# Delta-rule attention with routed experts: first scores from plain keys, small PSUM results in spare columns, routing in two stages

## The chip, the cores and the metric

The kernel runs on one core of a Trainium2 chip, in float32 throughout. The metric is device time in microseconds (us), less is better. Names of engines: PE is the tensor engine's matmul side and PEld its weight loads, DVE the vector engine, ACT the scalar engine, POOL the general engine, SP the engine whose queue issues most transfers. PSUM, where matmuls write, has eight banks of 512 float32 columns on 128 partitions.

## The reference

Two parts follow each other. The first is a delta-rule attention over 4 batches, 8 heads, 768 tokens, width 48; the second sends each of the 3072 tokens (8 heads side by side, 384 columns) to the one expert of eight with the highest logit.

```python
k_n = k / (norm(k) + 1e-6)
for t in range(S):
    y[:, :, t] = q[t] @ state
    v_old = state @ k_n[t]
    state = state + beta[t] * outer(k_n[t], v[t] - v_old)
x = y as (3072, 384)
logits = x @ w_gate
e = argmax(logits); gate = softmax(logits)[e]
out = gate * (relu(x @ w1[e]) @ w2[e])
```

## The kernel before

**The attention in chunks.** Tokens are handled in 24 chunks (steps) of 32 tokens, all four batches and eight heads of a chunk together: batch b lies on partitions 32b to 32b+31. For each chunk `scores` (L207) multiplies the keys with keys and queries into a PSUM tile `pa`, and `keep_scores` (L223) has DVE mask it into `gt` (keys) and `qk` (queries), two instructions on L235. Two heads share a partition range of 64 each, and to keep them apart the right-hand operand is a "wide" copy `wkq` with zeros in the other head's place, loaded by `load_wide` (L190) on top of the plain tile `kq`. There are three wide buffers, so a load of chunk c+3 waits for the matmuls of chunk c.

**The inversion.** Four chunks make a group. `invert` (L241) works on DVE alone: it normalises the keys, then inverts a triangular 32 by 32 matrix for each head, token and batch by about 30 pairs of a product (L324) and a sum (L329), and writes `ub` with four transposes (L336). It is a generator that yields after each instruction or two. For the first group only two 16-wide diagonal blocks are inverted, and the block across is made by PE: `across` (L350) multiplies (L358), ACT copies the result to `m` (L363), `second` multiplies again (L372) and DVE adds (L377). These are queued as chores.

**A step.** `begin(c)` (L407) takes the PSUM pair of banks `pc` and lets PE write the scaled values into its first bank (L411). `step(c)` (L417) then issues, in this order on PE: keys by state onto the same bank (L425), which ACT copies to R (L436); three transposes of the previous chunk's output (`turn`, L505); ub by R into the second bank of pc (L442), copied by ACT to Z (L447); queries by state into `pq` (L425); logits of the previous chunk (L521); sometimes one more score; qk by Z onto pq (L462), copied by ACT to `xg` (L472) and stored to the tensor xs; keys by Z onto the four banks `acc` (L478), from which ACT writes the states for the next step (L486). Between these ACT scales the next chunk's values (`scale_v`, L391). L425 of the next step needs the states.

**Who comes when.** The order on each engine is the order in which the Python code issues the instructions (the schedule is manual). `fill(us)` (L167) issues DVE instructions from the generators `soon` (routing) or `behind` (inversions) until an estimated number of microseconds is used up; two inversions at hand are issued in turn. The loop (L655 to L673) does a step, up to two chores, a score (`more`), `begin` of the next step, `fill(2.0)`, `fill(4.6)`, and only then the masks of that score. At each fourth step it first issues what is left of the inversion that the step needs (L656 to L658).

**PSUM.** acc takes four banks, pc two, pq one, and psA has one bank for everything else (L143): scores `pa`, the tile `po` of `across`, and the tile `pt` of `turn`, which holds the transposes, the logits (columns 384 to 391) and the ranks (from column 448). A new tile in psA waits until the one before has been read.

**Routing.** Once four chunks have logits (three and one at the end), `route` (L531) finds the best expert on DVE, has ACT take the exponential (L559) and makes the gate (L563 to L567, stored by SP on L568); `ranks` (L574) counts by two matmuls (L578), `listed` (L584) works out each token's place and POOL scatters the token numbers into lists (L605).

**The front.** Eight chunks (FRONT) are scored ahead of step 0, with a few matmuls without use (`heat`, L399) between. SP issues each key tile with its wide loads; values and keys by token of chunks 0 and 1 (`load_vt`, `load_kt`) are issued after the eight scores' loads (L646 to L648).

**The experts.** After the last step and its routing come 24 more heats, then for each expert a gather of its token rows on POOL (L722), transposes (L741), first product (L750), second product (L766) and a scatter of the output (L730).

Of the kernel before, what the change touches and what calls it, by code (L numbers as in the profile page):

```python
# [22 lines left out]
C = 32  # L23
# [17 lines left out]
FRONT = 8  # L41
RK = DM + 64
# [5 lines left out]
def _f32_consts():  # L48

    p = np.arange(128)[:, None]
    j = np.arange(128)[None, :]
    rev = np.broadcast_to(E - np.arange(E), (128, E))
    base = np.broadcast_to(np.arange(E) * LIST, (128, E))
    more = np.arange(E)[:, None] * LIST + CAP + np.arange(MAXR)[None, :] * 128
    more = np.broadcast_to(more.reshape(1, -1), (128, E * MAXR))
    t, w = p % C, j[:, :C]
    own = t // (C // 2) == w // (C // 2)  # L60
    kk = 1.0 * (t == w) - (t < w)
    k0 = 1.0 * (t == w) - ((t < w) & own) - (t // (C // 2) > w // (C // 2))
    return np.concatenate(
        [rev, base, more, p < j, np.ones((128, 128)), kk, k0, -1.0 * (t < w)], axis=1
    ).astype(np.float32)
# [3 lines left out]
def kernel(  # L69
# [22 lines left out]
    nc.scalar.dma_start(out=cf[:], in_=nc.inline_tensor(fc, name="c_f32").ap())  # L92
    at = [0]

    def part(w):
# [4 lines left out]
    rev, base, further, upper, ones, mask_g, mask_0, mask_q = (  # L100
        part(w) for w in (E, E, E * MAXR, 128, 128, C, C, C)
# [4 lines left out]
    nc.scalar.dma_start(out=wg[:], in_=moe_w_gate.rearrange("(s p) e -> p s e", p=128))  # L106
# [48 lines left out]
    beta = persist.tile([128, NG, C], FP32, name="beta")  # L155
# [3 lines left out]
    turned, counted, ranked = [], [], []  # L159

    behind, soon, chores = deque(), deque(), deque()
# [5 lines left out]
    def fill(us):  # L167


        while us > 0 and (soon or behind):  # L170
            from_ = soon or behind
            n = next(from_[0], None)
            if n is None:
                from_.popleft()
                continue
            us -= (0.09 if from_ is behind and len(behind) > 1 else 0.165) + 0.00104 * n
            if from_ is behind and len(behind) > 1:
                behind[0], behind[1] = behind[1], behind[0]

    def chore(n=1):  # L180
        while n and chores:
            chores.popleft()()
            n -= 1
# [6 lines left out]
    def load_wide(c):  # L190
        if c < NS:
            for e in range(2):

                r = slice(64 * e, 64 * e + (64 if c < 3 else D))
                nc.sync.dma_start(out=wide_kq[c % 3][r, e], in_=kq_t[c, r])
# [11 lines left out]
    def scores(c):  # L207

        if c >= NS:
            return None  # L210
        kq, wide = kqs[c], wide_kq[c % 3]
        pa = psA.tile([128, 512], FP32, name="pa", tag="pa")
        for p in range(NP):
            for b in range(B):
                nc.tensor.matmul(  # L215
                    pa[rows_of(b), 128 * p : 128 * p + 128], lhsT=kq[:, p, 0, rows_of(b)],
                    rhs=wide[:, :, p, :, rows_of(b)], start=True, stop=True, skip_group_check=True,
                )
        load_wide(c + 3)
        load_kq(c + 4) if c < FRONT - 4 else None  # L220
        return pa

    def keep_scores(c, pa):  # L223
# [6 lines left out]
        view = pa[:].rearrange("q (h k w) -> q k h w", h=H, k=2)  # L230
        for out, part, mask in (
            (gts[g][:, H * s : H * s + H, :], view[:, 0], mask_g if g else mask_0),
            (qks[c][:], view[:, 1], mask_q),
        ):
            nc.vector.tensor_tensor(  # L235
                out=out, in0=part, in1=mask.unsqueeze(1).to_broadcast([128, H, C]), op=OP.mult
            )
# [112 lines left out]
    def across(g, s):  # L350
# [3 lines left out]
        po = psA.tile([128, 512], FP32, name="po", tag="pa")  # L354
        for h in range(H):
# [8 lines left out]
            out=m1[:].rearrange("p h w -> p (h w)"), in_=po[:, 0 : H * W], func=AF.Copy  # L364
        )

        def second():
            po = psA.tile([128, 512], FP32, name="po", tag="pa")
            for h in range(H):
                sh = H * s + h  # L370
                for b in range(B):
                    nc.tensor.matmul(  # L372
                        po[rows_of(b), W * h : W * h + W], lhsT=fdt[rows_of(b), sh, :],
                        rhs=m1[rows_of(b), h, :], start=True, stop=True, skip_group_check=True,
                    )
            part = ub[:, H * s : H * s + H, W:C]
            nc.vector.tensor_tensor(  # L377
                out=part, in0=part,
                in1=po[:, 0 : H * W].rearrange("p (h w) -> p h w", h=H), op=OP.add,
# [19 lines left out]
    def heat(n=1):  # L399

        for _ in range(n):
            nc.tensor.matmul(  # L402
                front[0][:, 0, :], lhsT=ident[:],
                rhs=warm[:], start=True, stop=True, skip_group_check=True,
# [12 lines left out]
    def step(c):  # L417
# [15 lines left out]
        else:  # L433
# [5 lines left out]
            turn(c - 1)  # L439
        for h in range(H):  # L440
            for b in range(B):
# [3 lines left out]
                )  # L445
        Z = work.tile([128, H, D], FP32, name="Z")
# [7 lines left out]
        scale_v(c + 1, 0)  # L454
        if turned:
            logits(*turned.pop())
        if scored[0] < min(NS, c + LEAD):
            keep_scores(*score())
        scale_v(c + 1, 1)
        for h in range(H):  # L460
            for b in range(B):
                nc.tensor.matmul(  # L462
                    pq[rows_of(b), D * h : D * h + D], lhsT=qk[rows_of(b), h, :],
                    rhs=Z[rows_of(b), h, :],
                    start=(c == 0 and h == 0), stop=True, skip_group_check=True,
                )
        ss = first[c]
        if c == ss[0]:
            xgs[c] = work.tile([128, GS, ROW], FP32, name="xg")
            lgs[c] = small.tile([128, GS, E], FP32, name="lg")  # L470
        x = xgs[ss[0]][:, c - ss[0], 0:DM]
        nc.scalar.activation(out=x, in_=pq[:, 0:DM], func=AF.Copy, scale=-1.0)  # L472
        nc.sync.dma_start(out=xs[128 * c : 128 * c + 128, 0:DM], in_=x)
        if c < NS - 1:
# [9 lines left out]
            for e in range(2):  # L484
# [4 lines left out]
                )  # L489

# [9 lines left out]
    def turn(c):  # L500

        ss = first[c]
        pt = psA.tile([128, 512], FP32, name="pt", tag="pa")
# [5 lines left out]
        if counted:  # L509
            counted.pop()(pt)  # L510
# [4 lines left out]
        turned.append((c, xT, pt))  # L515

    def logits(c, xT, pt):

        ss = first[c]
        for s in range(NK):  # L520
            nc.tensor.matmul(  # L521
                pt[:, DM : DM + E], lhsT=xT[:, s, :], rhs=wg[:, s, :],
# [3 lines left out]
            out=lgs[ss[0]][:, c - ss[0], :], in_=pt[:, DM : DM + E], func=AF.Copy  # L526
# [4 lines left out]
    def route(ss, xg, lg):  # L531
# [6 lines left out]
        def wide(a):  # L538
# [23 lines left out]
        su = row("su", 1)  # L562
        nc.vector.tensor_reduce(out=su[:], in_=ex[:], axis=AX_X, op=OP.add)  # L563
        yield C
        nc.vector.tensor_scalar(out=su[:], in0=su[:], scalar1=1e-9, scalar2=None, op0=OP.add)
        yield C
        nc.vector.reciprocal(out=xg[:, 0:n, DM], in_=su[:])  # L567
        nc.sync.dma_start(  # L568
            out=xs.rearrange("(c p) r -> p c r", p=128)[:, ss[0] : ss[0] + n, DM],
            in_=xg[:, 0:n, DM],  # L570
        )
        yield C

        def ranks(pt):  # L574
# [7 lines left out]
            ranked.append(listed(pt))  # L582

        def listed(pt):  # L584
            pr = small.tile([128, 2 * GS * E], FP32, name="pr")
            nc.vector.tensor_copy(out=pr[:, 0 : 2 * n * E], in_=pt[:, RK : RK + 2 * n * E])
            yield C
# [26 lines left out]
    for c in range(GS):  # L614
        load_kq(c)
        if c < 3:
            load_wide(c)
    nc.scalar.dma_start(out=beta[:], in_=beta_blk)
    for t, eng in zip(wide_kq, (nc.vector, nc.gpsimd, nc.gpsimd)):
        eng.memset(t[0:64, 1], 0.0)  # L620
        eng.memset(t[64:128, 0], 0.0)
    nc.gpsimd.memset(warm[:], 0.0)
    nc.gpsimd.memset(states[:], 0.0)
    nc.gpsimd.memset(fdt[:], 0.0)
    nc.gpsimd.memset(empty[:], FAR)
    number = np.arange(128)[:, None] + 128 * np.arange(NS)[None, :]
    nc.scalar.dma_start(
        out=ids[:], in_=nc.inline_tensor(number.astype(np.int32), name="c_ids").ap()
    )
    nc.scalar.dma_start(out=lists.rearrange("(p s) o -> p (s o)", p=128), in_=empty[:])  # L630
    nc.vector.tensor_copy(out=cnt[:], in_=base)
    batch = {ss[-1]: ss for ss in BATCHES}
    first = {c: ss for ss in BATCHES for c in ss}
    front[0] = psC.tile([128, 2, 512], FP32, name="pc")
    for c in range(FRONT):
        if c >= GS:
            heat(2)
        keep_scores(*score())
        if c in (GS - 1, GS):
            fill(5.0)  # L640
        if c == GS + 1:
            heat(2)
            while not ubs:
                fill(0.1)
            chore(2)
    for c in range(2):  # L646
        load_vt(c)
        load_kt(c)  # L648
    for c in range(FRONT, LEAD + 2):
        load_kq(c)  # L650
    scale_v(0, 0)
    scale_v(0, 1)
    begin(0)
    pieces = deque()
    for c in range(NS):  # L655
# [3 lines left out]
        step(c)  # L659
        chore(2)  # L660
# [3 lines left out]
        fill(2.0)  # L664
        soon.extend(ranked)
        ranked.clear()
        fill(4.6)
# [6 lines left out]
    turn(NS - 1)  # L674
    logits(*turned.pop())
    fill(100.0)
    while counted:
        pt = psA.tile([128, 512], FP32, name="pt", tag="pa")
        counted.pop(0)(pt)
        soon.extend(ranked)  # L680
        ranked.clear()
        fill(100.0)
# [197 lines left out]
```

## Time and profile before

| | us |
|---|---|
| median of 3 runs (699.6 to 712.66) | 708.82 |
| the profiled execution, its time | 709.23 |
| its span | 707.5 |
| first L442 (step 0) starts at | 55.14 |
| L411 of step 4, 9 and 15 starts at | 124.5, 196.5, 270.1 |
| last step ends, tail begins | 356 |
| first transpose of the experts (L741) | 384.40 |
| busy PE, DVE, ACT, POOL over the span | 591.9, 230.3, 168.6, 105.5 |

Mean granted clock over the span: 0.896. A line of the timeline gives start, length, engine, line, operation, output<-input, shape and count; in square brackets is how long the engine stood idle ahead of it and what released it. A list of waits gives the engine and line that waited, what for, the total, the number of times and the longest. "Issue" is a wait for nothing that the profile shows. A float32 matmul has two records, so a count of 64 is 32 matmuls. The shares of the whole span mix three stages with different limits (the front up to 55, the steps up to 356 with the tail up to 384, the experts), so they are to be read by stage.

### The profile page before, as it was taken

The numbers are of one execution on the slowest core, as the hardware profiler recorded it, in microseconds if no ns is written. First come the engines' busy times: TensorE is split into PE (matmuls) and PEld (weight loads), VectorE is DVE, ScalarE is ACT, GpSimd is POOL, SyncE is SP. The second block draws the span as 40 slices with busy tenths as digits, with TensorE's granted clock in tenths as the row PEclk, the third lists the DMA queues.
The fourth block names the chain that finished last, engine by engine and source line by source line (L and its number), as shares of the span: only waits on it lengthen the run. The fifth ranks groups of instructions, "written<-read, shape, count | busy, mean of one in ns | idle before, by whom it ended". The sixth has DMA issues, their size and how long they took to land. (4 is left out here: it accounts for less than half of the span.)

```text
span 707.5 us, 17982 instructions
## 1 busy us (share of the span) xinstructions
PE 591.9 (84%) x7930; PEld 370.8 (52%) x7931; DVE 230.3 (33%) x780; ACT 168.6 (24%) x434; POOL 105.5 (15%) x111
## 2 busy tenths in 40 slices
PE   3655877568767869879989999999999999999991
PEld 2334655456655656566644555555455555555550
DVE  2740347758259378660131101011101111110200
ACT  0003223235435536555500101010101110110100
POOL 4000000001002001010234013141404031131011
PEclk9965557769879889997989999999999999999997
DMA  9928322337537424322103801243424232330000
GB/s 254 233 50 271 93 77 91 91 97 182 150 103 177 120 61 101 100 42 75 41 13 105 317 33 38 109 133 109 139 100 134 102 123 70 112 99 24 12 21 12
DMA packets 39505, 74.50 MB, mean 105 GB/s; under 512 B 10358, under 2 KB 24998, under 8 KB 39424
## 3 DMA queue, kind: packets, MB, share of 16 engines
q1 hardware_dynamic: 33840, 63.35, 30.9%
q0 software_dynamic: 4608, 9.47, 4.4%
q8 instruction: 63, 1.03, 0.7%
q10 hardware_dynamic: 976, 0.50, 0.4%
q14 instruction: 18, 0.15, 0.1%
HBM read 64.52 MB, written 10.35 MB: 106 GB/s over the span
## 5 line engine op out<-in xcount | busy, mean ns | idle before, releaser
L750 PE MATMUL phe<-xTe,w1t 128*128 128x448 f32 x384 | 146.5, 541 | 0.0
L766 PE MATMUL pye<-w2t,hT 128*128 128x384 f32 x384 | 125.2, 486 | 0.0
L750 PEld LDWEIGHTS phe<-xTe,w1t 128*128 128x128 f32 x384 | 72.3, 190 | 68.9 <-issue 67.1
L766 PEld LDWEIGHTS pye<-w2t,hT 128*128 128x128 f32 x384 | 73.0, 190 | 51.7 <-issue 3.0
L605 POOL DMA_INDIRECT lists<-ids,ri x24 | 23.8, 990 | 333.5 <-DVE ut L329 153.0
L755 DVE TENSOR_SCALAR hT<-phe 128x448 f32<-128x448 f32 x32 | 20.0, 625 | 125.6 <-PE phe L750 125.6
L730 POOL DMA_INDIRECT out_dram<-y,rows x24 | 24.0, 998 | 209.3 <-ACT y L775 175.9
L324 DVE TENSOR_TENSOR tmp<-ut 128x220 f32<-128x220 f32 (+12 forms) x164 | 51.4, 318 | 3.4
L329 DVE TENSOR_TENSOR ut<-ut,tmp 128x220 f32<-128x220 f32 (+12 forms) x164 | 51.5, 319 | 3.1
L215 PE MATMUL pa<-wkq,kq 128*32 128x128 f32 x768 | 35.7, 342 | 19.5 <-DMA wkq<-in_kq_t_dram 13.9
L759 ACT ACTIVATE hT<-phe 128x448 f32<-128x448 f32 x32 | 17.4, 543 | 140.4 <-PE phe L750 140.4
L391 ACT ACTIVATE vs<-vt,normt 128x48 f32<-128x48 f32 x192 | 47.7, 323 | 12.7 <-DMA vt<-in_v_tok_dram 12.7
L402 PE MATMUL pc<-warm,ident 128*128 128x512 f32 x88 | 49.4, 702 | 0.0
L486 ACT ACTIVATE states<-acc 48x768 f32<-48x768 f32 x46 | 37.0, 804 | 24.6 <-PE acc L478 24.0
L775 ACT ACTIVATE y<-pye,xin 128x384 f32<-128x384 f32 x16 | 9.3, 580 | 133.2 <-PE pye L766 133.2
L505 PE MATMUL pt<-ident,xg 128*128 128x128 f32 x72 | 15.3, 330 | 30.7 <-DVE qk L235 28.0
L215 PEld LDWEIGHTS pa<-wkq,kq 128*32 128x32 f32 x768 | 26.8, 136 | 27.0 <-issue 23.9
L745 DVE COPY xTe<-px 128x448 f32<-128x448 f32 x24 | 14.2, 614 | 77.2 <-PE px L741 77.1
L442 PE MATMUL pc<-R,ub 32*32 32x48 f32 x1472 | 25.6, 225 | 15.5 <-DVE ub L336 8.6
L478 PE MATMUL acc<-Z,kt 32*128 32x96 f32 x736 | 33.9, 327 | 3.3 <-issue 3.3
L442 PEld LDWEIGHTS pc<-R,ub 32*32 32x32 f32 x1472 | 21.7, 122 | 20.6 <-issue 16.3
L462 PE MATMUL pq<-Z,qk 32*32 32x48 f32 x1536 | 27.6, 227 | 5.2 <-issue 5.2
(102 smaller groups left out, 569.2 us busy)
## 6 DMA issues: line engine op xcount, KB each, us to landing
kq<-in_kq_t_dram SPq DMA_DIRECT2D x24, 512.0 KB, 6.3
w1t<-in_moe_w_dram SPq DMA_DIRECT2D x7, 1536.0 KB, 7.5
w2t<-in_moe_w_dram SPq DMA_DIRECT2D x7, 1536.0 KB, 7.0
wkq<-in_kq_t_dram SPq DMA_DIRECT2D x42, 192.0 KB, 5.1
kt<-in_k_tok_dram SPq DMA_DIRECT2D x24, 256.0 KB, 4.2
vt<-in_v_tok_dram SPq DMA_DIRECT2D x24, 192.0 KB, 3.5
xs<-xg SPq DMA_DIRECT2D x24, 192.0 KB, 3.5
wkq<-in_kq_t_dram SPq DMA_DIRECT2D x6, 256.0 KB, 6.6
```

Of the source, the lines that this page charges most:

```text
L215: nc.tensor.matmul(pa[rows_of(b), 128 * p : 128 * p + 128], lhsT=kq[:, p, 0, rows_of(b)], rhs=wide[:, :, p, :, rows_of(b)], start=True, st ...
L324: nc.vector.tensor_tensor(out=tv, in0=ud[:, :, j + 1 : W, j].unsqueeze(3).to_broadcast([128, K, n, j]), in1=ud[:, :, j, 0:j].unsqueeze(2). ...
L329: nc.vector.tensor_tensor(out=ud[:, :, j + 1 : W, 0:j], in0=ud[:, :, j + 1 : W, 0:j], in1=tv, op=OP.add)
L391: nc.scalar.activation(out=vss[c][:, h, :], in_=vts[c][:, h, :], func=AF.Copy, scale=norms[g][:, H * s + h : H * s + h + 1],)
L402: nc.tensor.matmul(front[0][:, 0, :], lhsT=ident[:], rhs=warm[:], start=True, stop=True, skip_group_check=True,)
L442: nc.tensor.matmul(pc[rows_of(b), 1, D * h : D * h + D], lhsT=ub[rows_of(b), H * s + h, :], rhs=R[rows_of(b), h, :], start=(h == 0), stop= ...
L462: nc.tensor.matmul(pq[rows_of(b), D * h : D * h + D], lhsT=qk[rows_of(b), h, :], rhs=Z[rows_of(b), h, :], start=(c == 0 and h == 0), stop= ...
L478: nc.tensor.matmul(acc[:, b, 96 * p : 96 * p + 96], lhsT=kt[rows_of(b), p, :], rhs=Z[rows_of(b), 2 * p : 2 * p + 2, :], start=(c == 0 and ...
L486: nc.scalar.activation(out=states[r, :, :, e], func=AF.Copy, scale=-1.0, in_=acc[r, :, 0:DM].rearrange("q b (p e w) -> q b p e w", p=NP, e ...
L730: nc.gpsimd.indirect_dma_start(out=out, out_offset=bass.IndirectOffsetOnAxis(ap=index, axis=0), in_=y[0:w, :], in_offset=None, bounds_chec ...
L750: nc.tensor.matmul(ph[:], lhsT=w1t[:, s, f * 128 : f * 128 + 128], rhs=xT[:, s, :], start=(s == 0), stop=(s == NK - 1),)
L766: nc.tensor.matmul(py[:], lhsT=hT[:, f, t * 128 : t * 128 + w], rhs=w2t[:, f, :], start=(f == 0), stop=(f == NF - 1),)
```

## The change

Line numbers with L and a number over 200 in the new code are those of the changed kernel where they are named together with its new order: its matmuls are L230 (plain scores), L242 (wide scores), L384 and L398 (across), L431 (heat), L439 (values), L453 (by state), L473 (ub by R), L492 (keys by Z), L511 (qk by Z), L538 (transposes), L558 (logits), L605 (ranks).

- The first six chunks (FRONT is 6) are scored from the plain tile: each head's 48 rows by themselves, 32 matmuls of 64 columns, into acc, which nothing uses before step 0; the two heads of a pair go to different banks, and two chunks are held at a time. Chunks 4 and 5 are scored ahead of the first inversion and masked after it. Wide loads begin with chunk 6.
- SP issues plain keys 0 to 5 with v and k by token of chunks 0 and 1 in between (after the fourth and the sixth), then keys 6 to 11 with the wide loads of 6 to 8. The constants come in two parts, masks and beta first.
- Only scores and heats use psA. `turn` writes its transposes into the first bank of pc, after R has been read, and stands behind L492 and the states; logits, ranks and the products of `across` use columns from 384 of the second bank of pc. Logits stand between L453 and L473; `scale_v` is issued earlier on ACT.
- In a step L492 and the states come ahead of L511.
- One extra score is issued in steps 0, 5 and 8 only (EXTRA); before, it was whenever fewer than c+10 chunks were scored.
- `fill` serves inversions only: 4.0 after the step, 2.8 after the next `begin`. Routing is issued whole by `urgent` between the two; its gate part is a generator of its own (`gates`), issued one step later; ranks are copied from PSUM by ACT instead of DVE. A chore is issued at three fixed places of a step, and the addition of `across` is a chore of its own.
- At the end, the last batch's routing is issued ahead of the list of the batch before it.

```diff
-FRONT = 8
-RK = DM + 64
+FRONT = 6
+EXTRA = (0, 5, 8)
+LG = DM
+RK = LG + E
...
+        if c < FRONT:
+            kq = kqs[c]
+            for p in range(NP):
+                for b in range(B):
+                    for e in range(2):
+                        r = slice(64 * e, 64 * e + D)
+                        nc.tensor.matmul(
+                            acc[rows_of(b), 2 * (c % 2) + e, 64 * p : 64 * p + 64],
+                            lhsT=kq[r, p, 0, rows_of(b)], rhs=kq[r, p, :, rows_of(b)],
+                            start=True, stop=True, skip_group_check=True,
+                        )
...
-        po = psA.tile([128, 512], FP32, name="po", tag="pa")
+        po = front[0][:, 1, DM:512]
...
             by_state(pc[:, 0, :], 0, False)
...
-            turn(c - 1)
+            logits()
+        scale_v(c + 1, 0)
...
+        chore()
         Z = work.tile([128, H, D], FP32, name="Z")
...
-        if scored[0] < min(NS, c + LEAD):
-            keep_scores(*score())
+        extra = score() if c in EXTRA else None
         scale_v(c + 1, 1)
...
+            if c:
+                turn(c - 1, pc[:, 0, :])
+            chore()
...
-    for c in range(FRONT):
-        if c >= GS:
-            heat(2)
-        keep_scores(*score())
...
+    begin(0)
+    for c in range(GS):
+        keep_scores(*score())
+    ahead = [score() for _ in range(GS, FRONT)]
+    heat(10)
+    while 0 not in ubs:
+        fill(0.1)
+    scale_v(0, 0)
+    scale_v(0, 1)
+    chore()
+    chore()
+    for a in ahead:
+        keep_scores(*a)
...
-        step(c)
-        chore(2)
+        extra = step(c)
+        fill(4.0)
+        if extra:
+            keep_scores(*extra)
+        chore()
+        urgent()
         more = score()
         if c + 1 < NS:
             begin(c + 1)
-        fill(2.0)
-        soon.extend(ranked)
-        ranked.clear()
-        fill(4.6)
+        fill(2.8)
         keep_scores(*more)
```

The new `urgent` and the new generator:

```python
    def urgent():
        for work_ in soon:
            for _ in work_:
                pass
        soon.clear()
        soon.extend(later)
        later.clear()
...
    def gates(ss, xg, ex):
        n = len(ss)
        su = small.tile([128, n], FP32, name="su")
        nc.vector.tensor_reduce(out=su[:], in_=ex[:], axis=AX_X, op=OP.add)
        yield C
        nc.vector.tensor_scalar(out=su[:], in0=su[:], scalar1=1e-9, scalar2=None, op0=OP.add)
        yield C
        nc.vector.reciprocal(out=xg[:, 0:n, DM], in_=su[:])
        nc.sync.dma_start(
            out=xs.rearrange("(c p) r -> p c r", p=128)[:, ss[0] : ss[0] + n, DM],
            in_=xg[:, 0:n, DM],
        )
        yield C
```

## The prediction

> **What bounds the kernel now.** I read the stage table first (each window: length, busy time with instruction counts of PE, PEld, DVE, ACT, POOL, then granted clock, DMA share, GB/s), then PE's waits by stage, then PE's instructions in order of time.
>
> ```profile
> 0.00:55.00 55.00, 26.39 (x404) 15.61 (x405) 24.43 (x79) 1.82 (x5) 7.37 (x15) 0.88 0.71 183
> 112.20:124.50 12.30, 9.65 (x271) 7.42 (x267) 11.65 (x48) 4.58 (x14) 0.00 (x0) 0.79 0.28 83
> 124.50:144.90 20.40, 11.79 (x272) 9.66 (x267) 12.49 (x52) 6.07 (x17) 0.00 (x0) 0.67 0.34 97
> 162.60:173.10 10.50, 8.26 (x272) 6.23 (x268) 8.39 (x32) 6.25 (x17) 1.00 (x1) 1.00 0.82 179
> 340.40:348.30 7.90, 7.59 (x238) 5.50 (x238) 0.00 (x0) 5.45 (x16) 1.92 (x3) 1.00 0.23 62
> 424.00:464.00 40.00, 39.92 (x132) 21.45 (x131) 6.65 (x13) 4.98 (x9) 9.33 (x9) 1.00 0.23 74
> ```
>
> From 384.4 us on (experts) PE is full at clock 1.00; the change doesn't touch that part: 707.5 - 384.4 = 323.1 us stay. Ahead of it the 24 steps (from 55.14 to 356) take 301 us, though a clean one takes 7.9 (window 340.4). PE's waits from 55 to 164, then from 164 to 356:
>
> ```profile
> PE pt L505 <- DVE qk L235: 10.9, 3, 5.8
> PE pc L442 <- DVE ub L336: 8.6, 1, 8.6
> PE pc L442 <- ACT vs L391: 4.9, 1, 4.9
> PE po L372 <- ACT m L363: 4.3, 3, 1.5
> ...
> PE pt L505 <- DVE qk L235: 17.1, 5, 6.4
> PE pc L442 <- issue: 5.6, 3, 2.4
> PE pq L462 <- issue: 5.2, 6, 1.3
> ```
>
> 28 us are transposes (L505) standing behind DVE's mask of the scores (L235): they share the one bank of psA, and DVE reaches the mask only after its share of the inversion and routing. "Issue" waits are about 17 us in the second list. A wait costs twice, as PE's order of time shows (start, length, instruction, wait ahead of it):
>
> ```profile
> 135.71 1.50 PE L442 MATMUL pc<-R,ub 32*32 32x48 f32 x64 [8.57 <-DVE ub L336]
> 137.14 1.51 PE L425 MATMUL pq<-states,kq 128*32 128x96 f32 x32
> 144.93 0.91 PE L411 MATMUL pc<-vs,ident 128*128 128x384 f32 x2
> 145.78 0.87 PE L425 MATMUL pc<-states,kq 128*32 128x96 f32 x32
> ```
>
> After the 8.57 us gap the same 32 matmuls take 1.51 us, and 0.87 once the clock is back, some 9 us later.
>
> **The change, part by part.** The sum is made against the profiled execution: span 707.5, time 709.23 (1.7 around it), median of the runs 708.82, 0.4 away.
>
> *A. Front (first L442 now at 55.14).* The first six scores read plain keys, so each needs 512 KB rather than 1 MB, and v, k of chunks 0 and 1 are queued on SP behind the fourth and sixth key tile, no longer behind wide loads that wait for PE (SP issued them at 51.13 to 52.97; ACT's scaling waited for them until 54.75). Worked out: transfers begin at about 2 us and the windows from 4 to 30 us move about 280 GB/s; four key tiles plus masks, beta and the late constants are 2.4 MB, 8.7 us, so 11 us. A score of 32 matmuls of 64 columns isn't in the trace: between 1.50 (32 of 48 columns, L442 slow) and 2.0; I take 1.93, the L215 row, with as many columns in all. Mask 0.75 and hand-over put DVE at 14. The first inversion ran from 22.39 to 41.47 with two masks of 0.75 inside: 17.6, so 31.6; the block products start one transpose (1.06) earlier and took 2.85 (40.70 to 43.55); the two held masks add part of 1.5. First L473 at 34. Ten heats (0.93 slow to 0.50 fast for each of two records: 10 to 18 us) lie under the inversion. A: 55.1 becomes 34.
>
> *B. Steps 0 to 3.* They took 69.4 (55.1 to 124.5). Removed: three L505 waits on DVE, the L391 wait, the 1.5 us waits for m (now the other products lie between the two halves). Clean step, by start-to-start times of fast rows: L439 0.84, L453 0.80, L558 0.80, L473 0.81, L453 0.80, L492 1.08, L538 0.47, L511 0.81, L242 1.01 = 7.4. Here a rule speaks against the change: the Trainium skill, "PSUM — Partial Sum Buffer", section "PSUM bank collisions raise a hardware error", says two engines may not be in one bank and quadrant together, even at other columns. Logits now sit in the bank that L473 writes, so L473 must wait for ACT's copy of them. The row (waits of DVE from 122 to 356):
>
> ```profile
> DVE pr L586 <- ACT lg L525: 16.6, 4, 5.1
> ```
>
> shows two reads of separate columns of one bank already kept in turn. Cost: L558's end to L473 is 0.08 + 0.18 + 0.06, 0.3 to 0.4 a step: 7.8, against 7.4 if only columns counted (8 us over 22 steps). I take 7.8. The rest of a step hides: states (1.63) lie under L538, L511, L242 and L439 (3.1); xT ends 0.1 to 0.2 ahead of the next L439, which writes its bank. If that cover is gone, each us late is a us a step. Steps 1 and 2 carry two products (2 x 0.7). With 0.5 of issue each: 9.7 + 9.7 + 8.3; step 0 is 6.0 of work, about 3.5 for the clock after 3 to 4 idle us, 0.6 for Z: 10.1. B: 69.4 becomes 37.8.
>
> *C. Step 4, a wait that returns.* The second inversion can start only when chunk 7 is masked, at the end of step 0; fills of 4.0 + 2.8 in steps 1 to 3 leave, in the changed program's order, ten multiply-add pairs (6.46 us, measured from 91.26 to 97.72), two scalings (1.1) and four transposes (1.9) to the start of step 4: 9.5. DVE starts 0.9 behind L242, PE comes to L473 after 2.8: wait 0.9 + 9.5 - 2.8 = 7.6. Queued behind L473: all of the step; ACT's Z waits with it. Then slow rows (1.43 + 1.43 + 1.96 + 0.8 + 1.43 + 1.86 = 8.9). By the skill's "TensorE: Matmul & The Clock Gate", Part 1, some 3.4 us of work would open the gate, 1.7 us lost; the trace shows 9 us, 4 lost. I use the trace. 2.8 + 7.6 + 8.9 = 19.3, was 20.4: nearly nothing gained.
>
> *D. Steps 5 to 7.* 38.3 before. The fifteen steps of before without the long waits (6 to 8, 10 to 12, 14 to 22, less their L505 waits) average 9.9: 7.9 clean, 1.1 issue, the rest slow clock after some issue waits. I keep 9.9, since nothing in the change removes those: 29.7 + 1.0 for an extra score: 30.7. Routing's first half no longer holds DVE in front of a mask, its second half (about 3.0) stands a step later.
>
> *E. Step 8, the same wait.* The third inversion starts at the end of step 4, and at step 8 its last 26 instructions alternate with the first 26 of the fourth: 9.5 + 7.4 alone, less 0.23 per pair (115.12 to 115.56 holds two, 0.67 alone): 11. Wait 0.9 + 11 - 2.8 + 1 of lag = 10.1; then 9.6. 22.5, was 13.3: a loss of 9.
>
> *F. Steps 9 to 14.* 73.6 before, with the 6.1 and 6.4 waits at steps 9 and 13. In the new order the fourth inversion ends in step 11, the fifth in 15, the sixth in 19, each before it is needed. DVE needs 7.2 + 0.75 + about 1.1 of routing, 9.0 a step, under 9.9. 6 x 9.9 = 59.4.
>
> *G, H.* Steps 15 to 22 keep their 78.2, step 23 and the tail (routing, four scatters, gathers, 24 heats) 36.1: the same chain, less a us at most.
>
> Edits at nothing: constants reordered and split on ACT's queue (done before 14 us), rank copies on ACT (0.23 in six steps; ACT is busy 5.5 of 9.9), memsets on POOL (done by 8.2 us, warm before the heats).
>
> Sum to the experts' start: 34 + 37.8 + 19.3 + 30.7 + 22.5 + 59.4 + 78.2 + 36.1 = 318.0, was 384.4. 707.5 - 66.4 = 641.1, plus 1.7: **643 us**.
>
> **Rivals.** *Leaner* (17%): issue waits and slow clock go with the long waits, and the 17 steps in D, F, G run like steps 12, 14, 15, 16 (8.0, 7.8, 8.5, 8.8, mean 8.3): 17 x 1.6 = 27 less, 616. For it: window 340.4. Against: issue waits fall in steps that had no other. *Given back* (22%): packed steps move their 1.8 MB in 8 to 10 us; window 162.6 has a share of 0.82 at 179 GB/s, so about 218 is full and 8.3 us a step is still under 9.9; but code comes by the same engines, and if issue waits double, with their slow clock, 1.8 x 17 = 30 more: 673. *Not what it says* (5%): xT, behind the states on ACT, holds the single pc buffer, and L439 waits 3 us in each of 22 steps: 66, 709. *Slower* (4%): the clock never opens. A 2.42 us gap at 188.8 was followed by slow rows, 2.2 at 216.6 wasn't; if each step holds an idle of over about 2.4 us, a step costs 7.8 x 1.78 = 13.9, 22 of them 306 instead of 208 here: about 740. It decides from about 16 such steps on.
>
> **How the numbers follow.** The case above has 52% (own range 628 to 658). The range 614 to 675 takes in the leaner case and the given-back one, and leaves the two others and the far tails. About 2% is what a measurement of this kernel tells from no change. Faster 0.91, same 0.05, slower 0.04.
>
> **What would show it.** First L473 near 34; no L538 wait on DVE; two waits of L473 on DVE ub, 7 to 8 and about 10 us, at steps 4 and 8 and none later; slow rows after them; L439 starts 8 to 10 us apart from step 9 on; experts' start near 318, length 323. Wrong if L439 waits on ACT, if issue waits exceed 2 us a step, or if the first L473 is past 45.

## The result and the profile after

The changed kernel takes 667.72 us (median of 4 runs, 663.11 to 673.95), the kernel before 706.79 beside it: ratio 0.946, 95% interval 0.934 to 0.958. Some executions of any of these kernels take over 1.5% longer than its fastest; the ratios leave them out, and where the profiled execution is one (660.1 us with two tiles, 659.06 with useless matmuls sized to the waits) only single rows and steps of it are read. The forecast was 643 with a range of 614 to 675: the direction and the range held, the likeliest value was 25 us too low. The range held in part by luck, since its upper end had been put there for a rival that did not happen. The profiled execution took 672.18 (span 670.4, mean clock 0.923), so the misses below add up to 29 and not to 25. The stages of the forecast, from the starts of the same matmuls in both profiles (us; step 4 begins with the values matmul, L411 before and L439 after):

| stage | before | forecast | after | missed by |
|---|---|---|---|---|
| A front, to the first ub by R | 55.1 | 34 | 34.1 | 0.1 |
| B steps 0 to 3 | 69.4 | 37.8 | 53.9 | 16.1 |
| C step 4 | 20.4 | 19.3 | 17.6 | -1.7 |
| D steps 5 to 7 | 38.3 | 30.7 | 35.1 | 4.4 |
| E step 8 | 13.3 | 22.5 | 20.9 | -1.6 |
| F steps 9 to 14 | 73.6 | 59.4 | 62.1 | 2.7 |
| G steps 15 to 22 | 78.2 | 78.2 | 80.1 | 1.9 |
| H step 23 and tail | 36.1 | 36.1 | 36.8 | 0.7 |
| experts | 323.1 | 323.1 | 329.9 | 6.8 |

The stage table of the kernel after (columns as before: window, length, busy PE, PEld, DVE, ACT, POOL, then clock, DMA share, GB/s):

```profile
34.10:88.00 53.90, 43.09 (x1404) 33.73 (x1404) 23.67 (x75) 20.10 (x55) 0.00 (x0) 0.72 0.36 108
88.00:105.60 17.60, 9.67 (x272) 7.86 (x268) 9.47 (x28) 5.33 (x16) 0.00 (x0) 0.71 0.27 81
140.70:161.60 20.90, 10.19 (x301) 8.39 (x300) 20.11 (x78) 5.13 (x15) 0.99 (x1) 0.76 0.34 91
161.60:223.60 62.00, 52.31 (x1610) 40.11 (x1610) 49.79 (x174) 33.87 (x95) 4.86 (x5) 0.94 0.54 146
```

In the first row PE is busy for 43.1 of 53.9 us at a clock of 0.72. The forecast for B held 31.0 us of work at full clock, 3.5 for slow clock and 3.3 of waits; so a good half of what B lost is slow work (8.6) and the rest idle time (10.8 instead of 3.3). In the second and third rows the idle part is the two waits that were forecast. PE's waits from 34 to 340 us (engine, what it writes, line, what released it; total, times, longest):

```profile
PE pc L558 <- ACT R L464: 10.3, 15, 1.7
PE pc L473 <- DVE tmp L350: 10.1, 1, 10.1
PE pc L473 <- DVE ub L362: 7.3, 1, 7.3
PE pc L473 <- ACT lg L562: 5.1, 19, 0.3
PE pc L398 <- ACT xT L543: 3.7, 2, 1.9
...
PE pc L439 <- ACT xT L543: 0.7, 2, 0.5
```

The 28 us of transposes behind DVE's mask are gone from the list: no L538 in it. The two single waits of 7.3 and 10.1 are steps 4 and 8. New, and not in the forecast, are the first row and that of L398. In PE's order of time (start, length, instruction, wait ahead of it) the first looks so in a step that has no other trouble:

```profile
205.60 0.87 PE L453 MATMUL pc<-states,kq 128*32 128x96 f32 x32
207.07 0.83 PE L558 MATMUL pc<-wg,xT 128*128 128x8 f32 x6 [0.61 <-ACT R L464]
208.18 0.88 PE L473 MATMUL pc<-R,ub 32*32 32x48 f32 x64 [0.27 <-ACT lg L562]
```

The logits (L558) need nothing of R, and lie in the other bank of the pair; yet they stand until ACT has read R out of the first. Then L473 waits 0.27 for the copy of the logits. This step takes 8.51 (204.75 to 213.26), where the forecast had 7.8.

### The profile page after: what moved, and what is told of

It is laid out like the page before. It is cut to its first block, busy times and chain, and to the rows that moved or that the text cites. A ratio compares the mean times of both kernels' runs of the same rounds, so it can differ in the third digit from the quotient of the medians.

```text
span 670.4 us, 18338 instructions
## 1 busy us (share of the span) xinstructions
PE 577.2 (86%) x8120; PEld 358.0 (53%) x8121; DVE 238.6 (36%) x773; ACT 169.2 (25%) x441; POOL 105.4 (16%) x111
## 3 DMA queue, kind: packets, MB, share of 16 engines
q1 hardware_dynamic: 33072, 60.99, 30.7%
q8 instruction: 64, 1.05, 0.7%
## 5 line engine op out<-in xcount | busy, mean ns | idle before, releaser
L790 PE MATMUL phe<-xTe,w1t 128*128 128x448 f32 x384 | 148.5, 547 | 0.0
L806 PEld LDWEIGHTS pye<-w2t,hT 128*128 128x128 f32 x384 | 73.0, 190 | 51.7 <-issue 3.0
L795 DVE TENSOR_SCALAR hT<-phe 128x448 f32<-128x448 f32 x32 | 20.0, 625 | 127.5 <-PE phe L790 127.5
L355 DVE TENSOR_TENSOR ut<-ut,tmp 128x58 f32<-128x58 f32 (+9 forms) x164 | 53.0, 323 | 4.8
L350 DVE TENSOR_TENSOR tmp<-ut 128x58 f32<-128x58 f32 (+9 forms) x164 | 52.7, 322 | 5.1
L473 PE MATMUL pc<-R,ub 32*32 32x48 f32 x1472 | 25.1, 222 | 24.0 <-DVE tmp L350 10.1
L431 PE MATMUL pa<-warm,ident 128*128 128x512 f32 x86 | 43.8, 655 | 0.0
L492 PE MATMUL acc<-Z,kt 32*128 32x96 f32 x736 | 33.3, 324 | 3.3 <-issue 3.3
L473 PEld LDWEIGHTS pc<-R,ub 32*32 32x32 f32 x1472 | 21.2, 119 | 26.9 <-issue 19.2
L558 PE MATMUL pc<-wg,xT 128*128 128x8 f32 x144 | 21.3, 268 | 13.9 <-ACT R L464 10.3
L492 PEld LDWEIGHTS acc<-Z,kt 32*128 32x128 f32 x736 | 28.8, 227 | 8.4 <-issue 6.1
L811 DVE TENSOR_SCALAR y<-pye,xin 128x384 f32<-128x384 f32 x8 | 4.9, 618 | 78.0 <-PE pye L806 78.0
L558 PEld LDWEIGHTS pc<-wg,xT 128*128 128x128 f32 x144 | 19.1, 202 | 18.6 <-ACT R L464 13.6
```

Source lines behind the costliest of these rows:

```text
L350: nc.vector.tensor_tensor(out=tv, in0=ud[:, :, j + 1 : W, j].unsqueeze(3).to_broadcast([128, K, n, j]), in1=ud[:, :, j, 0:j].unsqueeze(2). ...
L355: nc.vector.tensor_tensor(out=ud[:, :, j + 1 : W, 0:j], in0=ud[:, :, j + 1 : W, 0:j], in1=tv, op=OP.add)
L431: nc.tensor.matmul(pa[:], lhsT=ident[:], rhs=warm[:], start=True, stop=True, skip_group_check=True)
L473: nc.tensor.matmul(pc[rows_of(b), 1, D * h : D * h + D], lhsT=ub[rows_of(b), H * s + h, :], rhs=R[rows_of(b), h, :], start=(h == 0), stop= ...
L492: nc.tensor.matmul(acc[:, b, 96 * p : 96 * p + 96], lhsT=kt[rows_of(b), p, :], rhs=Z[rows_of(b), 2 * p : 2 * p + 2, :], start=(c == 0 and ...
L558: nc.tensor.matmul(pt[:, LG : LG + E], lhsT=xT[:, s, :], rhs=wg[:, s, :], start=(s == 0), stop=(s == NK - 1), skip_group_check=True,)
```

## The experiments

Each kernel ran beside the kernel before (median there 707.63 to 712.56 us), and ratios are to that. In the kernels with two tiles all lines lie 8 to 12 further down: L473 is L483 there, L558 is L568, L439 is L449, and the useless matmuls are L439 instead of L431.

**One pair of banks as two tiles.** Theory: the waits of L558 for R, and of L398 for xT, come from the pair being declared as one tile. Rival: they come of the banks, or are covered anyway.

```diff
-        front[0] = psC.tile([128, 2, 512], FP32, name="pc")
+        front[0] = Pair(
+            psC.tile([128, 512], FP32, name="pc"), psC.tile([128, 512], FP32, name="pd")
+        )
```

> The pair of banks pc is declared as two tiles of one bank each; nothing else changes. Theory 'one tile': logits (L558) stand 0.61 us behind ACT's R and the block product (L398) 1.85 us behind ACT's xT only because they share a tile with what ACT reads, though not a bank. Then both waits go: a clean step falls from 8.5 to about 7.9 us, steps 1 and 2 lose 1.85 us each and some slow clock, in all 22 x 0.6 + 4 to 8 = 17 to 21 us less than the changed kernel (about 648). Rival 'bank': the waits come from ACT being in the way or from the logits' own input; then the waits stay and the time is 668 within 5.

Measured: 651.34 (647.06 to 660.1), ratio 0.919 (0.914 to 0.925), 16 us under the changed kernel by the medians and 19 by the two ratios. A clean step of it:

```profile
200.65 0.87 PE L463 MATMUL pc<-states,kq 128*32 128x96 f32 x32
201.45 0.83 PE L568 MATMUL pd<-wg,xT 128*128 128x8 f32 x6
202.55 0.88 PE L483 MATMUL pd<-R,ub 32*32 32x48 f32 x64 [0.27 <-ACT lg L572]
```

The 0.61 is gone, the 0.27 stays; the step takes 7.94 (199.70 to 207.64), 0.57 less. The same PSUM banks, columns and order, so it was the declaration. In the changed kernel the waits for R sum to 13.3 us (10.3 on L558, and 3.0 on L605 where ranks come first); what is left is within the intervals.

**The second product ahead of the transposes.** In steps 1 and 2 the second product of the block across (L398) stood 1.85 and 1.82 us behind ACT's copy xT.

```diff
+            chore()
             if c:
                 turn(c - 1, pc[:, 0, :])
-            chore()
```

> In a step the block product's second half (L398) is issued ahead of the transposes, not behind them; nothing else changes. If the wait for xT is what slows steps 0 to 3 (53.9 us against 37.8 foretold), the two waits of 1.85 us go and the clock holds through steps 2 and 3: 6 to 10 us less. Rival 'clock': the slow stretch comes from the gaps at step 0 (issue waits of 1.5 us) and from small waits; then 2 to 4 us less, and slow rows stay in step 3.

Measured: 668.47, ratio 0.941 (0.935 to 0.947), no different from 0.946. The wait for xT is gone, but in step 1 PE then stands 2.8 us at the next score instead. The two-tile kernel, which has no such wait either, shows the same place:

```profile
55.06 0.86 PE L521 MATMUL pq<-Z,qk 32*32 32x48 f32 x62
59.84 1.82 PE L250 MATMUL pa<-wkq,kq 128*32 128x128 f32 x32 [3.91 <-DMA xs<-xg]
```

The releaser named is a store that the score does not read. Counting PE's matmul records from the start of the trace, this gap stands at record 1241; in the changed kernel 0.88 us (put down to DVE) stand at the same record:

```profile
58.70 1.94 PE L242 MATMUL pa<-wkq,kq 128*32 128x128 f32 x32 [0.88 <-DVE normt L324]
```

The larger gaps without a cause come at records 221, 349, 604, 858, 1241 in the changed kernel, and at 221, 349, 476, 604, 732, 986 in a kernel whose front has other instructions (the last one below): steps of about 128 records or a multiple, whatever instruction stands there. The score starts at 58.7 us in the changed kernel, at 58.4 without the wait for xT, and at 58.0 and 59.8 in two executions with two tiles. So the wait for xT hid a stop of PE's own stream; its removal only showed the stop.

**Useless matmuls in the two long waits.** Are the rows after them slow because PE idled?

```diff
         scale_v(c + 1, 0)
+        if c in (4, 8):
+            heat(14 if c == 4 else 18)
```

> Ahead of L473 PE gets 14 matmuls without use at step 4 and 18 at step 8, about 7 and 9 us, to lie in the waits for DVE (7.3 and 10.1 us). If slow clock after the waits costs what the rows say (L473 to L242 8.0 us instead of 5.5 at step 4, and 8.0 instead of 6.5 at step 8, plus a slow first half of the heats which the wait hides), 4 to 6 us less than the changed kernel. Rival: the clock there costs nothing in the end because DVE is late anyway at the next point: no change within 2 us.

Measured: 673.78, ratio 0.950 (0.946 to 0.955): nothing gained. The number of heats was wrong, since one `heat` is two records:

```profile
89.43 12.26 PE L431 MATMUL pa<-warm,ident 128*128 128x512 f32 x28
101.62 0.88 PE L475 MATMUL pc<-R,ub 32*32 32x48 f32 x64
102.43 0.87 PE L453 MATMUL pq<-states,kq 128*32 128x96 f32 x32
```

14 heats took 12.3 us against a wait of 7.3. The rows after them ran fast, though: 5.1 us from L475 to the next step (101.62 to 106.71) instead of 7.2 (98.41 to 105.57). With the right size, on the two-tile kernel (`heat(7 if c == 4 else 10)`):

> The two one-bank tiles (651 us, 0.919 of the kernel before) with useless matmuls ahead of ub by R at steps 4 and 8, now sized to the wait: 7 of 0.9 us (6.3) at step 4 and 10 (9.0) at step 8. If the idle clock is what makes the rows after the two waits slow: the waits show as 1 us or less, both steps keep their length up to ub by R, the rows after it run at about 0.8 instead of 1.4 us, 2 to 4 us less at each: 645, ratio 0.910. If the clock there is withheld for another reason: rows still 1.4, 651, ratio 0.919.

Measured: 649.18, ratio 0.919 (0.915 to 0.922), against 0.919 without. The mechanism shows in rows (ub by R at step 4 in 1.05 us instead of 1.50, step 4 itself 16.4 instead of 17.3 us, step 8 20.5 instead of 21.8, the longer times each from the two-tile kernel with the longer tail below), but the 2 us that this makes are less than the interval. The slow rows after a wait are a small term.

**Eight chunks in the front.** If the waits at steps 4 and 8 come of the late start of the second inversion, chunks 6 and 7 in the front should remove them. First with all masks but two ahead of the first inversion (`FRONT = 8`, six masks first):

> Eight chunks instead of six are scored from plain keys, six masked ahead of the first inversion, so the second inversion can start in step 0 instead of step 1. Theory 'late start': the waits of 7.3 and 10.1 us at steps 4 and 8 exist because an inversion starts only one step after its group's last score; both shrink by the 6.8 us of fill that a step has, the front grows by 1.5 to 4 us: 8 to 12 us less. Rival 'DVE is full': the two waits move to later steps or come back elsewhere, since DVE has no more room: within 3 us of the changed kernel.

Measured: 668.23, ratio 0.940 (0.935 to 0.946). The wait at step 4 fell from 7.28 to 3.9 and that at step 8 from 10.08 to nothing, and the way from the first ub by R to step 9 from 127.5 to 113.8 us; but the first ub by R came at 42.76 instead of 34.11, 8.65 later. Of this, 7.6 are the inversion, which started at 21.40 instead of 13.81, behind the masks of chunks 4 and 5; the rest is the useless matmuls, which ended 1.9 us after the transposes that L384 reads (0.8 in the changed kernel). On the two-tile kernel with the inversion started ahead of those masks:

```diff
-FRONT = 6
+FRONT = 8
...
-    ahead = [score() for _ in range(GS, FRONT)]
+    ahead = [score() for _ in range(2)]
+    fill(8.0)
+    for a in ahead:
+        keep_scores(*a)
+    ahead = [score() for _ in range(2)]
     heat(10)
```

> The two one-bank tiles with chunks 6 and 7 also scored from plain keys in the front, the first inversion started ahead of the masks of chunks 4 and 5, so that the second inversion can start in step 0 rather than step 1. If the waits of ub by R on DVE at steps 4 and 8 come from the late start of the inversions: front 1.5 us longer (two pairs of masks), the wait at step 4 falls from 7 to under 2 and that at step 8 from 10 to under 2, with 2 us of slow rows less at each: 636 to 640, ratio 0.90. If the transfers of two more key tiles hold the front up, as when eight were masked ahead of the inversion (8.65 us): 645 to 648, ratio 0.913.

Measured: 650.7, ratio 0.917 (0.912 to 0.923). Again the front was long (first ub by R at 43.45), and this time the trace names the cause. The front of it in PE's order:

```profile
28.87 0.85 PE L238 MATMUL acc<-kq 48*32 48x64 f32 x36 [3.81 <-issue]
29.65 11.56 PE L439 MATMUL pa<-warm,ident 128*128 128x512 f32 x20
41.15 0.72 PE L392 MATMUL pd<-ub,gt 32*32 32x16 f32 x64
```

DVE had finished the inversion's last transpose at 33.5 us; the ten useless matmuls, which before filled the inversion, now started 8 us later, behind the scores of chunks 6 and 7, and ran until 41. The cover had become the wait. The key tiles are not what held up the scores: the 3.81 us stand in the middle of chunk 7's matmuls (record 476).

**The front alone.** The kernel before with nothing changed but the front (six chunks from plain keys, the loads of v and k among them):

> The kernel before with the front alone changed: six chunks scored from plain keys into acc, v and k of chunks 0 and 1 issued among them; steps, psA, turn, logits, routing and fills as before. By the sum, first ub by R at 34 instead of 55 and the rest as before: 709 - 21 = 688, ratio 0.970. If the earlier start is given back in steps 0 to 4 (the second inversion starts with less done ahead and step 4 waits longer for it): 695 to 705, ratio 0.98 to 0.995.

Measured: 694.55, ratio 0.981 (0.975 to 0.986): 13 us, not 21. The first ub by R is at 34.07, exactly as in the changed kernel, but step 4 pays:

```profile
123.04 1.50 PE L455 MATMUL pc<-R,ub 32*32 32x48 f32 x64 [16.13 <-DVE ub L349]
```

8.57 had stood there before. From the first ub by R to step 5 it takes 98.5 us instead of 89.8: 8.7 of the 21 are given back at the second inversion, which starts with less done ahead. The other changes together are worth the remaining 25 of the 39 us that the whole change brings (0.981 to 0.946); how much each of them brings was not tried apart.

**A longer cover at the tail.** In the changed kernel the last heats end only 4.0 us after the first gather is issued (336.50 to 340.5; before, 6.15), and SP's weight loads, which wait for them, are issued at 340.75, among the gathers. The tail of the changed kernel:

```profile
318.23 22.44 PE L431 MATMUL pa<-warm,ident 128*128 128x512 f32 x48
340.51 0.27 PE L781 MATMUL px<-ident,xin 128*128 128x128 f32 x1
...
342.34 0.33 PE L781 MATMUL px<-ident,xin 128*128 128x128 f32 x1 [1.03 <-DMA xin<-xs,rows]
345.55 2.63 PE L781 MATMUL px<-ident,xin 64*128 64x64 f32 x9 [2.88 <-DMA xin<-xs,rowh]
```

On the two-tile kernel with `heat(28)` for `heat(24)`:

> The two one-bank tiles with 28 instead of 24 useless matmuls ahead of the experts (3.8 us more of them). If the gathers are late because the weight loads that the last useless matmul sets free run against them: gathers land in about 3 us, the 5.6 us of waits for rows fall to under 1 and the transposes run fast; 3.8 later, 5 to 6 earlier: 649, ratio 0.916, with the first transpose about 330.7 and the first product within 3 us of it instead of 9. If the gathers are slow by themselves (four of them in a row on one queue): they land at 333.5 as before, the useless matmuls only fill the wait, 650 to 651, and the gathers' median stays at 6.

```profile
299.99 27.14 PE L439 MATMUL pa<-warm,ident 128*128 128x512 f32 x56
326.96 2.16 PE L791 MATMUL px<-ident,xin 128*128 128x128 f32 x12
329.06 18.31 PE L800 MATMUL phe<-xTe,w1t 128*128 128x448 f32 x48
```

No wait for rows is left, and the experts take 322.4 us (span 649.4 less 326.96) instead of 329.9, as before the change (323.1). In the time it does not show: 651.06, ratio 0.921 (0.916 to 0.926), against 0.919. 7.5 us of experts are bought with 4.7 of heats; the net 3 is inside the interval.

**Is it the key loads that make PE stop?** The two-tile kernel with the keys of chunks 6 to 8 kept and used for all later chunks (loads of keys from chunk 9 on left out):

> The two one-bank tiles (651 us, 0.919) with the key loads left out from chunk 9 on: keys of chunks 6 to 8, plain, wide and by token, stay and are used again for all later chunks, so steps load values and weights only (that part of the computation is changed). If the issue waits (some 20 us over the steps) are code that comes late because the key loads hold the same engines: they fall to under 6 us in all, and with them slow rows, 15 to 25 us less: 626 to 636, ratio 0.89. If PE stops at every 128th matmul record whatever is loaded: issue waits 15 us or more and 646 to 651, ratio 0.915 to 0.92.

Measured: 721.92, ratio 1.014 (1.008 to 1.020). As a time this says nothing of the stops. The steps got shorter (the last heats start at 284.07 instead of 299.99), but with other tokens routed the experts took much longer: their first transposes came 23 us after the heats, as the first gather was issued only at 327.75, after 17 us of waiting for its lists, and 34 us of idle time stand ahead of a further gather at the end that the other kernels don't have. How the changed routing brings the late lists was not followed up. Read by stage, first this kernel, then the two-tile kernel with `heat(28)`, the same two stretches of steps:

```profile
96.00:132.00 36.00, 30.08 (x965) 23.13 (x953) 31.09 (x111) 20.10 (x57) 3.82 (x4) 1.00 0.37 86
150.00:290.00 140.00, 128.76 (x3710) 96.14 (x3702) 91.15 (x343) 79.66 (x227) 17.60 (x18) 0.94 0.24 56
```

```profile
96.00:132.00 36.00, 29.89 (x963) 22.99 (x955) 26.00 (x92) 19.50 (x53) 3.07 (x3) 0.98 0.70 184
150.00:290.00 140.00, 124.91 (x3709) 93.54 (x3702) 93.34 (x328) 80.30 (x223) 13.62 (x14) 0.94 0.46 113
```

The DMA share halves. The stops without a cause over the steps (one that the profile puts down to a store among them) sum to 11.5 us instead of 20.3: 4.5 instead of 12.3 from 54 us after the first step on, but 7.0 instead of 8.0 in the first 54. Neither expectation holds: in the later steps the stops shrink by two thirds when the load halves (three two-tile kernels with all loads have 11.5 to 13.5 us there), in the first steps they don't, though the DMA share halves there too (0.37 to 0.19 in steps 0 to 3).

A count speaks for code. The page of the changed kernel lists a queue of kind "instruction":

```profile
q8 instruction: 64, 1.05, 0.7%
```

These are 64 packets and 1.05 MB. PE ran 8120 matmuls and 8121 weight loads in that execution, 254 to a packet, or 127 matmul records: the spacing of the stops. With 7930 matmul records (the kernel before) there are 63 packets, with 8184 (the kernel with 14 and 18 heats) 65. So PE's code most likely comes in such packets, and a stop is one that came late; what made it late was not shown.

**The parts together.** Two tiles, eight chunks in the front with `heat(2)` for `heat(10)` there, and `heat(28)` at the tail:

> The two one-bank tiles, eight chunks from plain keys with the first inversion started ahead of the masks of chunks 4 and 5, but 2 instead of 10 useless matmuls in the front, and 28 ahead of the experts. The run with 10 of them (650.7 us) had PE busy with them for 9 us after the inversion was done. If that was its loss: first ub by R at 35 to 36 instead of 43.5, wait at step 4 about 4 to 5 us and none at step 8, rows for the experts there when PE asks: 638 to 643, ratio 0.905. If the front is held by chunk 7's scores or a slow clock instead: first ub by R at 40 or later, 646 to 650, ratio 0.915.

Measured: 641.74 (639.65 to 645.86), ratio 0.903 (0.898 to 0.908), the fastest of all. The front of it, and the wait of step 4:

```profile
29.21 0.85 PE L238 MATMUL acc<-kq 48*32 48x64 f32 x36 [4.08 <-issue]
29.99 3.78 PE L439 MATMUL pa<-warm,ident 128*128 128x512 f32 x4
33.70 0.82 PE L392 MATMUL pd<-ub,gt 32*32 32x16 f32 x64
...
92.60 1.50 PE L483 MATMUL pd<-R,ub 32*32 32x48 f32 x64 [4.56 <-DVE tmp L358]
```

First ub by R at 37.06, 1 to 2 us later than expected; step 4 waits 4.56, step 8 not at all, and the experts take 323.2. Against the run with ten heats (650.7) the first ub by R comes 6.4 us earlier for eight heats less, so the overshoot was most of that loss; the rest of the 9 us includes the four heats more at the tail, which weren't tried apart here.

## Why the forecast was right in direction and 25 us too low

*A, the front: right,* 34.1 for 34, and by its own steps: DVE started the inversion at 13.81 (forecast 14) and ended it at 31.88 (31.6). The ten heats did not lie wholly under it, though: PE had stopped for 5.21 us ahead of them, and they ended at 31.9, 0.8 us after L384 could have started.

*C and E, the two returning waits: right in place and size.* 7.28 for 7.6 and 10.08 for 10.1. The term beside them was too dear: I took 9 us of slow rows after such a wait from one place of the profile before (after the 6.14 us wait at 204.34 of that profile they were slow for about 5.5), and set the shorter warm-up of the Trainium skill aside ("TensorE: Matmul & The Clock Gate", Part 1, about 3.4 us of work). The rows now:

```profile
98.41 1.50 PE L473 MATMUL pc<-R,ub 32*32 32x48 f32 x64 [7.28 <-DVE ub L362]
...
101.28 1.95 PE L492 MATMUL acc<-Z,kt 32*128 32x96 f32 x32
103.16 0.55 PE L538 MATMUL pc<-ident,xg 128*128 128x128 f32 x3
```

They are slow for 4.75 us here and for 4.2 after the wait of step 8 (153.93 to 158.10), nearer the page than the 9 us of the profile before, so both steps came out 1.6 to 1.7 shorter in spite of a logits wait of 0.6.

*The clean step: wrong.* "L558's end to L473 is 0.08 + 0.18 + 0.06, 0.3 to 0.4 a step: 7.8" counted the wait of L473 for the logits (0.27 measured) and took for granted that L558 runs while ACT copies R. It does not, as the pair of banks is one tile: 8.51. The steps of D, F and G carried a clean step of 7.9 inside their 9.8 to 9.9; 0.6 more in each of the 17 makes 10 us, where these stages missed by 9.0 together. The two-tile kernel shows the step at 7.94. The weighing of columns against banks missed this wait, for which the declared tile decided; for the 0.27 it stays open, since the logits and the output of L473 share a bank and a tile in both kernels. The row for it (DVE pr L586 <- ACT lg L525) could not tell either, as ranks and logits lay in one tile `pt`.

*B, steps 0 to 3: wrong,* and the largest term, 16.1. With two tiles the stage takes 48.1 (34.92 to 83.01, the kernel with the longer tail), 5.8 less. But four executions with one tile and unchanged first steps, or nearly so, lie between 50.5 and 53.9 (mean 51.7) and three with two tiles between 48.1 and 49.4 (48.7), so only about 3 are the one tile, waits for xT among them. In the execution of 48.1, 10.3 over the forecast, 6.5 are stops: 8.0 us of them, where "with 0.5 of issue each" allowed 1.5 for three steps. The remaining 3.8 lie in slow rows: I allowed 3.5 us for the clock in step 0 only, and the clock over the stage is 0.79 there and 0.72 in the changed kernel. I had taken the quiet late steps as the model of early ones. Why the clock stays low in step 3, which has hardly a wait in it, and why the stops are dense here even without key loads, stays open.

*The experts: wrong at "stay",* 6.8. The part was untouched, but its first weight loads start when the heats ahead of it end, and the change let these end sooner after the first gather: gathers and weight loads met. The longer cover brings the part to 322.4.

*The rivals.* "Given back" came nearest in number (673) but not in mechanism: stops without a cause did not double, they sum to 14.7 us from 34 to 316 us, where before they were 20.0 over the steps (19.5 to 22.0 in three two-tile kernels with all loads). "Leaner" is out: the 17 steps average 10.4, where it needed 8.3. "Not what it says" is out as a cost: L439 did wait for ACT's xT, which the forecast had named as a sign of being wrong, but in two steps only and for 0.26 and 0.46 us, not 3 us in each of 22. "Slower" is out: the clock opens again after each wait, and is 0.94 in steps 9 to 14. Of the other signs, the steps from 9 on did not keep to 8 to 10 us: seven of the fourteen took 10.4 to 12.4.

## What to carry to other kernels

Before counting an instruction as hidden, ask of the declared tile, not only of the bank or columns, who reads or writes it last: a reader of one bank and a writer of the other were kept in order here because both banks were one tile. A cover of useless work has a length and a start; when what precedes it moves, measure again whether it still ends first (in three kernels here it ended last by 1.9 us or more, and once too early for the transfers behind it). A stage that the change does not touch still has a beginning that the change moves.

## What the runs showed of the hardware

PE stopped for up to 6.0 us (in the front of the kernel with six masks first) at matmul records about 128 or a multiple of it apart, whatever instruction stood there, and the profile names a bystander or "issue" for it; a wait at the same place hides it. Not every gap without a cause lies there: some of 0.2 to 0.7 us fall between. In the later steps the gaps without a cause shrank from 12.3 to 4.5 us in all when the DMA share halved. That the stops are code coming late is likely from the count of packets; no run changed the code's transfer alone.
